# GEGLU feed-forward on one core: two small reads ahead of ScalarE's first block of x

## The chip, the cores and the metric

The kernel runs on one core of a Trainium2 chip. A core has five engines with instruction streams of their own: TensorE (PE, matmuls; its weight loads are shown apart as PEld), VectorE (DVE), ScalarE (ACT), GpSimd (POOL) and SyncE (SP), which here only starts transfers. Transfers started by SP and by ScalarE go through one DMA queue each (q1 and q10 in the profile); GpSimd's go through q0. All of them are carried out by the core's 16 DMA engines. Engines order themselves by semaphores. The metric is device time in microseconds, the median of several runs; less is better.

## What is computed

x has 1024 rows of 1024 (32 x 32 tokens), w_gate and w_up are 1024 x 3584, w_down is 3584 x 1024, all in bf16:

```python
def reference(x, w_gate, w_up, w_down):
    return (_gelu(x @ w_gate) * (x @ w_up)) @ w_down
```

`_gelu` is the tanh form of GELU.

## The kernel before

Every instruction stream is written out by hand: one function for each engine (`prog_sp`, `prog_act`, `prog_pool`, `prog_pe`, `prog_dve`) issues its instructions in order, and `wait` puts a semaphore wait ahead of the next one. There is no scheduler; the order on an engine is the order of the text. Each group of transfers has a semaphore of its own, wrapped in a `_Clock` that counts to 16 for one transfer.

*The work.* The hidden dimension, 3584, is cut into 28 chunks of 128 (`m`); the contraction over 1024 into 8 steps of 128 (`dk`). TensorE multiplies a 128 x 128 tile of weights with up to 512 columns of the transposed x (`xT`) and collects the 8 steps in a PSUM bank, once for the gate (G) and once for the up projection (U) (L388). ScalarE puts GELU on G (L446), VectorE multiplies it with U into `hT` (L486). After all chunks, TensorE runs the second product from `hT` and `wd` (L425), and ScalarE and VectorE take turns at copying the result out.

*The start.* x comes with its rows on the partitions and must be transposed. The first 256 rows come as two blocks of 128 rows and 256 KB, `xa[:, 0]` by SP and `xa[:, 1]` by ScalarE (L293, in `early_loads`, whose argument `side` is 0 for SP and 1 for ScalarE). For `dk` 0 to 4 TensorE transposes them by multiplying with an identity matrix (L355, `turn_xa`), in the order: block 0 for dk 0 to 2, block 1 for dk 0 to 2, block 0 for dk 3 and 4, block 1 for dk 3 and 4; ScalarE copies the three results from PSUM to `xT` (L439). For `dk` 5 to 7 VectorE transposes both blocks in 16 instructions (L462), after waiting for both. Ahead of this, TensorE runs seven matmuls of 512 columns on constants (`WARM`, L402), whose result is not used.

*The early weights.* After its block of x, SP starts the first 1024 columns (8 chunks) of both weight tensors, one `dk` at a time: wg and wu for k = 0, then for k = 1, and so on (L289, `load_w0`), 256 KB each, the last pair in halves. The weight tensors are laid out with 8 consecutive rows on each partition, so block k takes from every partition's group of 8 rows the row k. TensorE's first real matmuls are the 8 chunks for dk = 0 on the first 256 columns of x, in an order of parts and keys that follows the PSUM banks that the transposes leave free; then dk = 1 to 5 for all 8 chunks, and so on.

*The rest of x.* The remaining rows of x are started as six pieces by SP and six by ScalarE (L284, `load_x`), once the wu block for k = 5 has landed; on ScalarE they stand behind the three copies of L439. VectorE transposes them (L477). Later weights are started by SP (wg) and GpSimd (wu), L278 and L272.

At its end SP waits for the last output transfer.

Of the kernel before, what the change touches and what calls it, by code (L numbers as in the profile page):

```python
# [5 lines left out]
P = 128  # L6
BF16 = mybir.dt.bfloat16
# [77 lines left out]
def bass_standalone__geglu_ffn__sampling_kernel(  # L85
# [119 lines left out]
    def evac_eng_is_act(ji):  # L205
        return ji % 2 == 0
# [18 lines left out]
    Q_WD_SP = _Clock("wd_sp", 16)  # L225
    Q_WD_POOL = _Clock("wd_pool", 16)
    Q_OUT = _Clock("out", 16)
    all_clocks = [C_PE, C_ACT, C_DVE, C_POOL, *Q_XA, *Q_X.values(), *Q_W0.values(), *Q_W7.values(), *Q_WG, *Q_WU,
                  Q_WD_SP, Q_WD_POOL, Q_OUT]

    ctx = _Ctx()

    with ExitStack() as es:
        def sb(name, shape, dtype):
            return es.enter_context(nc.sbuf_tensor(name, shape, dtype))
# [11 lines left out]
        w_r = {"wg": wg_r, "wu": wu_r}  # L247
        NTB = 4
        t_bufs = [sb(f"tb{i}", [P, 512], FP32) for i in range(NTB)]
        warm = sb("warm", [P, 2], FP32)  # L250
        assert TC * D == DK * N
        osb = xT
        ps = es.enter_context(nc.psum_tensor("ps", [P, 8, 512], FP32))
# [13 lines left out]
        def issue_wd(ew, eng, mine, upto_chunk, clock, force=False):  # L267
            for k in list(mine):
                if force or wd_gate_chunk[k] <= upto_chunk:
                    ew.wait(C_PE, ctx.get(("U", last_part[wd_gate_chunk[k]])))  # L270
                    a, b = wd_groups[k]
                    ew.do(lambda: eng.dma_start(wd[:, a:b, :], wd_r[:, a:b, :]), clock=clock)  # L272
                    mine.remove(k)

        def load_w(ew, eng, w, j):
            c0, gsz, buf = groups[j]
            q = (Q_WG if w == "wg" else Q_WU)[j]
            ctx.set((w, j), ew.do(lambda: eng.dma_start(  # L278
                wbuf(w, buf)[:, :, 0:gsz * P], w_r[w][:, :, c0 * P:(c0 + gsz) * P]), clock=q))

        def load_x(ew, eng, q, side):
            c0, c1 = q[0] // 32, q[1] // 32
            for a in (2 * side, 2 * side + 1):
                v = ew.do(lambda: eng.dma_start(  # L284
                    xs[32 * a:32 * (a + 1), c0:c1, :], x_r[a, :, c0:c1, :]), clock=Q_X[(q, side)])
            ctx.set(("x", q, side), v)

        def load_w0(ew, eng, w, k, f0, f1, q):
            ctx.set((w + "0", k, f0), ew.do(lambda: eng.dma_start(  # L289
                big[w][:, k, f0:f1], w_r[w][:, k, f0:f1]), clock=q))  # L290

        def early_loads(ew, eng, side):
            ctx.set(("xa", side), ew.do(lambda: eng.dma_start(  # L293
                xa[:, side, :], xa_r[:, side, :]), clock=Q_XA[side]))
            yield
            if side == 0:
                for k in range(DK - 1):
                    for w in ("wg", "wu"):
                        load_w0(ew, eng, w, k, 0, NBIG * P, Q_W0[(w, k)])
                for h in range(2):  # L300
                    for w in ("wg", "wu"):
                        load_w0(ew, eng, w, DK - 1, h * GSZ * P, (h + 1) * GSZ * P,
                                Q_W7[w] if h else Q_W0[(w, DK - 1)])
            ew.wait(Q_W0[("wu", 5)], ctx.get(("wu0", 5, 0)))
            for q in XPIECES:
                load_x(ew, eng, q, side)

        def gate_w(ew, j):
            if war[j] is None:
                for s in range(2):  # L310
                    ew.wait(Q_X[(XC2, s)], ctx.get(("x", XC2, s)))
                return -1
            ew.wait(C_PE, ctx.get(("U", last_part[war[j]])))
            return war[j]
# [15 lines left out]
        def prog_sp(eng):  # L330
            sp = _Eng(ctx, eng, None)
            for _ in early_loads(sp, eng, 0):
                pass
            wd_mine = [k for k in range(len(wd_groups)) if k % 2 == 0]
            for j in range(NG):
                known_chunk = gate_w(sp, j)
                load_w(sp, eng, "wg", j)
                issue_wd(sp, eng, wd_mine, known_chunk, Q_WD_SP)
            issue_wd(sp, eng, wd_mine, FM, Q_WD_SP, force=True)
            ctx.set("wd_sp_total", Q_WD_SP.n)  # L340
            last = None
            for ji, (tc, col0, ncols, b) in enumerate(jobs):
                sp.wait(C_ACT if evac_eng_is_act(ji) else C_DVE, ctx.get(("E", ji)))
                last = sp.do(lambda: eng.dma_start(
                    out_r[:, tc, col0:col0 + ncols],
                    osb[:, tc, col0:col0 + ncols]), clock=Q_OUT)
            sp.wait(Q_OUT, last)

        def turn_xa(pe, eng, b, dk):
            pe.wait(Q_XA[b], ctx.get(("xa", b)))  # L350
            j = next(j for j, (_, k0, k1) in enumerate(XA_PS) if k0 <= dk < k1)
            bank, k0, k1 = XA_PS[j]
            o = 256 * (dk - k0) + P * b
            last = dk == k1 - 1 and b == 1
            v = pe.do(lambda: eng.matmul(  # L355
                ps[:, bank, o:o + P],
                xa[:, b, :].rearrange("p (j k) -> p j k", k=DK)[:, :, dk],
                ident[:, :], start=(dk == k0 and b == 0), stop=last), mark=last)
            if last:
                ctx.set(("XP", j), v)  # L360
# [72 lines left out]
        def prog_act(eng):  # L433
            act = _Eng(ctx, eng, C_ACT)
            act.do(lambda: eng.activation(warm[:, 0:1], const0, ACTF.Gelu_apprx_tanh))
            for _ in early_loads(act, eng, 1):
                for j, (bank, k0, k1) in enumerate(XA_PS):
                    act.wait(C_PE, ctx.get(("XP", j)))
                    ctx.set(("XA", j), act.do(lambda: eng.activation(  # L439
                        xT[:, k0:k1, XA[0]:XA[1]],  # L440
                        ps[:, bank, 0:256 * (k1 - k0)].rearrange("p (k t) -> p k t", t=256), ACTF.Copy)))
            for i, (m, t0, t1, (gb, g0, g1), us) in enumerate(parts):
                act.wait(C_PE, ctx.get(("U" if us[0] == gb else "G", i)))
                if i >= NTB:
                    act.wait(C_DVE, ctx.get(("D", i - NTB)))
                ctx.set(("A", i), act.do(lambda: eng.activation(  # L446
                    t_bufs[i % NTB][:, 0:t1 - t0], ps[:, gb, g0:g1], ACTF.Gelu_apprx_tanh)))
            for ji, (tc, col0, ncols, b) in enumerate(jobs):
                if not evac_eng_is_act(ji):
                    continue  # L450
                act.wait(C_PE, ctx.get(("O", ji)))
                ctx.set(("E", ji), act.do(lambda: eng.activation(  # L452
                    osb[:, tc, col0:col0 + ncols], ps[:, b, 0:ncols], ACTF.Copy)))

        def prog_dve(eng):
# [38 lines left out]

        progs = [
            (prog_sp, nc.sync, "sync"),
            (prog_act, nc.scalar, "scalar"),
            (prog_pool, nc.gpsimd, "gpsimd"),
# [45 lines left out]
```

## Time and profile before

| | |
|---|---|
| median of 3 runs | 299.84 us (299.69 to 299.94) |
| the profiled execution | 299.69 us |
| its span, first to last instruction | 298.4 us |
| TensorE busy | 294.2 us, 99% |
| VectorE, ScalarE, GpSimd busy | 64.3, 42.2, 7.9 us |
| moved from and to memory | 24.12 MB read, 2.10 MB written |
| ScalarE's queue, q10 | 1776 packets, 1.05 MB |

The span leaves out what lies ahead of the first and behind the last instruction, 1.3 us here. TensorE is busy for nearly all of the span; the row of busy tenths in 40 slices shows it at 9 (90% or more) in all but the first slice (8) and the last (7). A matmul is pipelined, so the length given for one is longer than the distance to the next one; distances between starts tell the rate. Rows of the timeline that end in `q` (SPq, ACTq) are the issues of transfers, and their length is the time that issuing takes, not that of the transfer.

### The profile page before, as it was taken

The page shows a single profiled execution, that of the slowest core. Times are in us where ns is not written, and L with a number is a line of the kernel's source. Part 1 is how long each engine was busy: PE and PEld are TensorE (multiplying, and loading weights), DVE is VectorE, ACT ScalarE, POOL GpSimd, SP SyncE. Part 2 cuts the span into 40 slices and gives each one's busy share as a digit, 9 for nine tenths or more (in the row PEclk, how much of TensorE's full clock was granted, in tenths as well). Part 3 has the DMA queues.
Part 4 walks back from the last instruction along what each step waited for, and adds up shares of the span by engine and source line. Part 5 has one row for each costly group of instructions (what it writes and reads, how often), then busy time and mean ns, then how long its engine had stood idle before and what let it go on. Part 6 is the DMA issues. An engine that isn't in the chain of part 4 may idle for free.

```text
span 298.4 us, 3487 instructions
## 1 busy us (share of the span) xinstructions
PE 294.2 (99%) x1525; PEld 149.3 (50%) x1549; DVE 64.3 (22%) x108; ACT 42.2 (14%) x78; POOL 7.9 (3%) x14
## 2 busy tenths in 40 slices
PE   8999999999999999999999999999999999999997
PEld 5899644444444444444444444444444444444446
DVE  4669722111122111122111112110000000000000
ACT  3032211121111121111112111110000000000000
POOL 1001001020001002001000000000000000000000
PEclk9999999999999999999999999999999999999999
DMA  7997104856008301942104000000000100010001
GB/s 255 386 205 234 51 2 125 296 181 244 0 0 295 129 0 27 371 167 93 49 0 141 0 2 0 0 0 20 18 18 18 37 18 18 20 35 18 18 20 35
DMA packets 18094, 26.43 MB, mean 89 GB/s; under 512 B 1056, under 2 KB 11936, under 8 KB 18080
## 3 DMA queue, kind: packets, MB, share of 16 engines
q1 hardware_dynamic: 14128, 16.78, 17.3%
q0 software_dynamic: 2176, 8.39, 7.9%
q10 hardware_dynamic: 1776, 1.05, 1.4%
q8 instruction: 12, 0.20, 0.3%
q14 instruction: 2, 0.02, 0.0%
HBM read 24.12 MB, written 2.10 MB: 88 GB/s over the span
## 4 chain that ended last, share of the span: by engine, by line
PE 99%; issue 0%; ACT 0%
PE ps L388 65%; PE ps L425 32%; PE ps L402 1%; PE ps L355 0%; ACT xT L452 0%
## 5 line engine op out<-in xcount | busy, mean ns | idle before, releaser
L425 PE MATMUL ps<-wd,hT 128*128 128x512 bf16 (+1 forms) x468 | 96.5, 366 | 0.4
L388 PE MATMUL ps<-xT,wgbig 128*128 128x512 bf16 (+2 forms) x394 | 79.6, 337 | 0.3
L388 PE MATMUL ps<-xT,wubig 128*128 128x512 bf16 (+2 forms) x395 | 79.5, 336 | 0.3
L425 PEld LDWEIGHTS ps<-wd,hT 128*128 128x128 bf16 x476 | 46.6, 98 | 50.4
L486 DVE TENSOR_TENSOR hT<-tb,ps 128x512 bf16<-128x512 f32 (+1 forms) x64 | 38.9, 615 | 136.6 <-PE ps L388 136.6
L446 ACT ACTIVATE tb<-ps 128x512 f32<-128x512 f32 (+1 forms) x64 | 34.2, 544 | 158.3 <-PE ps L388 155.4
L388 PEld LDWEIGHTS ps<-xT,wgbig 128*128 128x128 bf16 x400 | 38.3, 98 | 31.7 <-DMA wgbig<-in_w_gate_dram 0.2
L388 PEld LDWEIGHTS ps<-xT,wubig 128*128 128x128 bf16 x400 | 38.1, 98 | 31.4
L388 PE MATMUL ps<-xT,wgsmall 128*128 128x512 bf16 x126 | 30.1, 379 | 0.1
L388 PE MATMUL ps<-xT,wusmall 128*128 128x512 bf16 x125 | 29.8, 379 | 0.2
L492 DVE CAST xT<-ps 128x512 bf16<-128x512 f32 (+1 forms) x8 | 5.3, 658 | 88.1 <-PE ps L425 88.1
L388 PEld LDWEIGHTS ps<-xT,wgsmall 128*128 128x128 bf16 x128 | 12.5, 98 | 15.1
L388 PEld LDWEIGHTS ps<-xT,wusmall 128*128 128x128 bf16 x128 | 12.5, 98 | 15.1
L452 ACT ACTIVATE xT<-ps 128x512 bf16<-128x512 f32 (+1 forms) x9 | 5.2, 573 | 93.1 <-PE ps L425 93.1
L477 DVE STREAM_TRANSPOSE xT<-hT 128x128 bf16<-128x128 bf16 (+2 forms) x20 | 13.4, 705 | 0.0
L462 DVE STREAM_TRANSPOSE xT<-hT 32x192 bf16<-32x192 bf16 x16 | 8.2, 514 | 4.7 <-DMA hT<-in_x_dram 4.2
L278 POOL DMA_DIRECT2D wubig<-in_w_up_dram x3 | 2.7, 884 | 62.9 <-PE ps L388 62.9
L402 PE MATMUL ps<-const-bfloat16-1.0 128*128 128x512 bf16 x7 | 3.1, 627 | 0.8 <-PEq L529 0.8
L278 POOL DMA_DIRECT2D wusmall<-in_w_up_dram x2 | 2.0, 993 | 47.9 <-PE ps L388 26.0
L272 POOL DMA_DIRECT2D wd<-in_w_down_dram x3 | 2.3, 766 | 19.1 <-PE ps L388 19.1
L402 PEld LDWEIGHTS ps<-const-bfloat16-1.0 128*128 128x128 bf16 x7 | 0.9, 139 | 2.1 <-issue 2.1
L439 ACT ACTIVATE xT<-ps 128x512 bf16<-128x512 f32 (+1 forms) x3 | 1.4, 527 | 2.4 <-PE ps L355 2.4
(10 smaller groups left out, 4.9 us busy)
## 6 DMA issues: line engine op xcount, KB each, us to landing
wd<-in_w_down_dram SPq DMA_DIRECT2D x4, 1024.0 KB, 11.3
wgbig<-in_w_gate_dram SPq DMA_DIRECT2D x3, 1024.0 KB, 5.8
wubig<-in_w_up_dram POOLq DMA_DIRECT2D x3, 1024.0 KB, 9.6
wd<-in_w_down_dram POOLq DMA_DIRECT2D x3, 1024.0 KB, 11.3
wgsmall<-in_w_gate_dram SPq DMA_DIRECT2D x2, 1024.0 KB, 5.9
wusmall<-in_w_up_dram POOLq DMA_DIRECT2D x2, 1024.0 KB, 9.7
out_dram<-xT SPq DMA_DIRECT2D x15, 128.0 KB, 1.7
wgbig<-in_w_gate_dram SPq DMA_DIRECT2D x7, 256.0 KB, 5.3
```

Source lines behind the costliest of these rows:

```text
L272: ew.do(lambda: eng.dma_start(wd[:, a:b, :], wd_r[:, a:b, :]), clock=clock)
L278: ctx.set((w, j), ew.do(lambda: eng.dma_start(wbuf(w, buf)[:, :, 0:gsz * P], w_r[w][:, :, c0 * P:(c0 + gsz) * P]), clock=q))
L388: v = pe.do(lambda: eng.matmul(ps[:, bank, f0:f1], wbuf(w, buf)[:, dk, slot * P:(slot + 1) * P], xT[:, dk, t0:t1], start=first, stop=last ...
L402: pe.do(lambda: eng.matmul(ps[:, 0, 0:n], ones_w, ones_x[:, 0:n], start=True, stop=True), mark=False)
L425: v = pe.do(lambda: eng.matmul(ps[:, b, 0:ncols], hT[:, m, tc * P:(tc + 1) * P], wd[:, m, col0:col0 + ncols], start=(m == 0), stop=(m == F ...
L439: ctx.set(("XA", j), act.do(lambda: eng.activation(xT[:, k0:k1, XA[0]:XA[1]], ps[:, bank, 0:256 * (k1 - k0)].rearrange("p (k t) -> p k t", ...
L446: ctx.set(("A", i), act.do(lambda: eng.activation(t_bufs[i % NTB][:, 0:t1 - t0], ps[:, gb, g0:g1], ACTF.Gelu_apprx_tanh)))
L452: ctx.set(("E", ji), act.do(lambda: eng.activation(osb[:, tc, col0:col0 + ncols], ps[:, b, 0:ncols], ACTF.Copy)))
L462: v = dve.do(lambda: eng.transpose(xT[32 * a:32 * (a + 1), XA_DVE[0]:XA_DVE[1], XA[0]:XA[1]].rearrange("p k (b t) -> p k b t", t=P)[:, :, ...
L477: v = dve.do(lambda: eng.transpose(xT[:, dk, q[0]:q[1]].rearrange("p (c i) -> p c i", i=32), src))
L486: ctx.set(("D", i), dve.do(lambda: eng.tensor_tensor(hT[:, m, t0:t1], t_bufs[i % NTB][:, 0:t1 - t0], ps[:, ub, u0:u1], ALU.mult)))
L492: ctx.set(("E", ji), dve.do(lambda: eng.tensor_copy(osb[:, tc, col0:col0 + ncols], ps[:, b, 0:ncols])))
```

## The change

On ScalarE's side, `early_loads` first starts two small transfers: the first 16 columns (32 bytes) of each of the 128 rows of block k = 0 of `w_up`, then the same of `w_gate`, into a new small tile `probe`. Nothing reads this tile. Only then is ScalarE's block of x started. The order of the text on ScalarE is thus: the activation that loads the table, probe of `w_up`, probe of `w_gate`, block 1 of x, the three copies, the later pieces of x. The two transfers share a new semaphore, and SP waits for it at the very end, behind its wait for the last output. The rows read are those of the first wu and wg blocks that SP starts behind its own block of x. No other instruction is added, removed or moved.

```diff
+    Q_PROBE = _Clock("probe", 16)
     all_clocks = [C_PE, C_ACT, C_DVE, C_POOL, *Q_XA, *Q_X.values(), *Q_W0.values(), *Q_W7.values(), *Q_WG, *Q_WU,
-                  Q_WD_SP, Q_WD_POOL, Q_OUT]
+                  Q_WD_SP, Q_WD_POOL, Q_OUT, Q_PROBE]
...
+        probe = sb("probe", [P, 2, 16], BF16)
...
         def early_loads(ew, eng, side):
+            if side == 1:
+                for i, w in enumerate(("wu", "wg")):
+                    v = ew.do(lambda: eng.dma_start(probe[:, i, :], w_r[w][:, 0, 0:16]), clock=Q_PROBE)
+                ctx.set("probe", v)
             ctx.set(("xa", side), ew.do(lambda: eng.dma_start(
                 xa[:, side, :], xa_r[:, side, :]), clock=Q_XA[side]))
             yield
...
             sp.wait(Q_OUT, last)
+            sp.wait(Q_PROBE, ctx.get("probe"))
```

## The prediction, made before the changed kernel had run

> **What bounds the kernel now.** I read the chain of waits first. It is TensorE from end to end, so the time is the moment at which TensorE begins to run without a break, plus a fixed row of matmuls.
>
> ```profile
> PE 99%; issue 0%; ACT 0%
> PE ps L388 65%; PE ps L425 32%; PE ps L402 1%; PE ps L355 0%; ACT xT L452 0%
> ```
>
> Idle time in front of L388 and L425 is 0.1 to 0.4 us per group on the page. No later stall can be gained back, so only the first microseconds can move, and I read those next, in the timeline (start, length, engine, line, operation).
>
> ```profile
> 0.73 0.39 SPq L293 DMA_DIRECT2D hT<-in_x_dram  x1
> 0.77 3.15 PE L402 MATMUL ps<-const-bfloat16-1.0 128*128 128x512 bf16 x7 [0.77 <-PEq L529]
> 0.78 0.38 ACTq L293 DMA_DIRECT2D hT<-in_x_dram  x1
> ...
> 1.17 0.42 SPq L289 DMA_DIRECT2D wgbig<-in_w_gate_dram  x1
> ...
> 1.64 0.42 SPq L289 DMA_DIRECT2D wubig<-in_w_up_dram  x1
> ...
> 3.96 1.03 PEld L355 LDWEIGHTS ps<-ident,hT 128*128 128x128 bf16 x10 [0.96 <-issue]
> ...
> 4.24 8.13 DVE L462 STREAM_TRANSPOSE xT<-hT 32x192 bf16<-32x192 bf16 x15 [4.24 <-DMA hT<-in_x_dram]
> ...
> 4.65 1.36 ACT L439 ACTIVATE xT<-ps 128x256 bf16<-128x256 f32 x3 [2.43 <-PE ps L355]
> ...
> 5.18 1.08 PEld L388 LDWEIGHTS ps<-xT,wgbig 128*128 128x128 bf16 x7 [0.18 <-DMA wgbig<-in_w_gate_dram]
> ...
> 7.26 0.86 PEld L388 LDWEIGHTS ps<-xT,wgbig 128*128 128x128 bf16 x8
> ```
>
> Seven warm-up matmuls fill TensorE until 3.92. From 3.96 it transposes x (L355): rows of block 0 (SP's), then of block 1 (ScalarE's), dk 0 to 2 of each, then dk 3 and 4. ScalarE copies the first product out from 4.65 to 5.03, and the first real matmul starts at 5.18. When the blocks land is in the DMA view of 1.16 to 2.43 us (last column: us from issue to landing):
>
> ```profile
> q1 hardware_dynamic: 40, 0.08, 39.5%
> issues: line engine op xcount, KB each, median us to landing
> ...
> hT<-in_x_dram ACTq DMA_DIRECT2D x1, 256.0 KB, 3.4
> wubig<-in_w_up_dram SPq DMA_DIRECT2D x1, 256.0 KB, 4.2
> ```
>
> ScalarE's block of x lands at 0.78 + 3.4 = 4.18, and wu's k=0 block at 1.64 + 4.2 = 5.84. The first wg block has the shortest landing of that tile, 4.0 us, so 1.17 + 4.0 = 5.17, just before the start at 5.18. Narrow windows of the weight loads put the fourth transpose, the first that needs block 1, at 4.20. So block 1 has no slack to its own use, and the chain behind it has about 0.10 us: the copy ends at 5.03, TensorE could go on at 5.08, and it waits for wg until 5.18.
>
> One more thing is in these rows. The granted clock reads 1.00 in every stretch, but the starts do not: the warm-up loads follow each other by 0.42 us for 512 columns, while at 7.26 eight matmuls of 256 columns take 0.87 us, or 109 ns each. Narrow windows of the first L388 loads show 0.21 us for 256 columns up to 6.02 and half of that from there:
>
> ```profile
> 5.59 0.36 PEld L388 LDWEIGHTS ps<-xT,wgbig 128*128 128x128 bf16 x2
> ...
> 5.80 0.35 PEld L388 LDWEIGHTS ps<-xT,wgbig 128*128 128x128 bf16 x2
> ...
> 6.02 0.25 PEld L388 LDWEIGHTS ps<-xT,wgbig 128*128 128x128 bf16 x2
> ```
>
> TensorE thus runs at half rate until about 6.05, 5.28 us after its first matmul and after a spell with under 0.4 us of idle time in it.
>
> **The change, part by part.** *Two more DMA issues on ScalarE's queue.* SP's issues start 0.46 us apart (1.17, 1.64, 2.10), so block 1 is issued at 0.78 + 2 x 0.46 = 1.70 and not at 0.78. ScalarE itself has nothing to do until 4.65 but its table load, so the issues cost it nothing directly. Behind them on the queue come only block 1, the copies of L439, and the later pieces of x (held until 12.7 by a weight landing).
>
> *Whom block 1 now stands behind.* The issue order was SP x, ScalarE x, wg, wu. It becomes SP x, probe wu, wg (1.17), probe wg (1.24), wu (1.64), ScalarE x (1.70). Does ScalarE's queue wait for SP's older transfers? The row that shows it is at 12.71, where both queues issue pieces of x at the same moment, SP behind six blocks of weights still under way, ScalarE behind nothing:
>
> ```profile
> 12.71 3.90 SPq L284 DMA_DIRECT2D hT<-in_x_dram  x6
> 12.71 3.91 ACTq L284 DMA_DIRECT2D hT<-in_x_dram  x6
> ```
>
> The DMA view of 12.71 to 14.6 holds 643 packets of q1 (SP) and none of q10 (ScalarE); in 14.6 to 15.4 both move:
>
> ```profile
> q1 hardware_dynamic: 643, 0.68, 108.0%
> ...
> q1 hardware_dynamic: 269, 0.14, 76.2%
> q10 hardware_dynamic: 146, 0.07, 38.5%
> ```
>
> ScalarE's empty queue waited 1.9 us, as long as SP's own. The start agrees: SP's block of x moves its first packets 1.0 us after its issue, ScalarE's, issued 0.05 us later, has none before 2.43. I read this as service in the order of issue over both queues. Block 1 then moves from second to fourth place among blocks of 256 KB, the place that lands at 5.84. The probes add 256 packets, 16 for each DMA engine. Their price is not in the trace; between the 4-byte packets (9 ns) and the 512-byte ones (27 to 35 ns) it is 0.14 to 0.55 us, and I take 0.2, nearer to the small ones. Against this, two neighbours on different queues interleave (the two x blocks landed 0.3 us apart, where weight blocks are 0.67 apart), so I take off 0.3: 5.84 + 0.2 - 0.3 = 5.7. Ends: 4.7 (no service in issue order, below) and 6.4 (no interleaving, dear probes).
>
> [...]
>
> *TensorE's start.* Block 1 is 5.7 - 4.18 = 1.52 late; 0.10 of it is taken by the slack, so the first real matmul starts 1.42 later, at 6.60. wg has landed by then. The 0.87 us of work that TensorE did at half rate between 5.18 and 6.05 was worth 0.43 us at full rate; if the full rate still came at 6.05, the net loss would be 1.42 - 0.43 = 0.99 us.
>
> *The half rate.* TensorE now stands idle from 4.32 (three transposes of block 0) to 5.76, inside the spell that led to the full rate. No row shows what such a gap does. Below: idle time merely does not count, and the full rate comes 1.52 later, at 7.57; from 6.60 that is 0.97 us at half rate, a loss of 0.49. Above: the 5.28 us begin anew at 5.76 and end at 11.04; 4.44 us at half rate, a loss of 2.22. I take the middle, 9.3: 2.70 us, a loss of 1.35. The sum is 0.99 + 1.35 = 2.34 us.
>
> [...]
>
> *What stays hidden.* DVE's 16 transposes (L462) start with block 1 as well, 4.24 to about 5.8, and end at 14.5 instead of 12.95. TensorE needs them for dk=5 at 14.2 before, which moves to 16.5 in the forecast and to 15.2 at the least delay of 0.99; if that cover were gone, TensorE would wait for the difference. ScalarE's three copies then end at 7.53, and the matmuls that need the last one come 1.5 us behind the first at half rate, so about 8.1. Weight blocks and the other pieces of x move by the probes alone, 0.2 us, against over 1 us of new slack. SP's last wait finds its semaphore long reached: 0 to 0.05 us (one "issue" step of the chain), taken as 0.
>
> The profiled execution took 299.69 us with a span of 298.4; the forecast span is 300.7, that execution 302.0. The median is 0.15 above it, so 302.2 us.
>
> **The rivals.**
> 1. *Queues share, block 1 is hardly late* (not slower). Place: ScalarE's DMA queue. Its packets start 1.0 us after its issue as SP's first did, at 2.7 instead of 2.43, and it lands at 4.7 to 5.1 because q1 takes every second turn. The start slips 0.4 to 0.8 us, all within the half-rate spell, which halves it: 0.2 to 0.4, so 300.1. For it: 0.3 us between the two landings at the start. Against it: 12.71. It decides as long as block 1 lands before about 5.3; at that landing the loss reaches 0.6.
> 2. *Block 1 is late, but the full rate comes at 6.05 all the same*: + 0.99, 300.8. For it: nothing in the trace counts idle time. Against it: warm-up work alone, up to 3.92, did not bring the full rate, so a spell is being judged.
> 3. *The spell begins anew*: 0.99 + 2.22 = 3.21, 303.1.
> 4. *The early reads help the first weight blocks*. In 4.8 to 5.2 the DMA engines moved 246 GB/s and not the 385 of 2.43 to 3.1, so wg's landing could come sooner. TensorE waits for wg only 0.10 us, so this can't give more than 299.7, and only if block 1 were not late. This is also why a clear gain has almost no room.
>
> **How the numbers follow.** Forecast (302.2, with its own range 301.3 to 302.9) 0.45; rival 1 0.17; rival 2 0.24; rival 3 0.10; rival 4 or anything faster 0.04. 0.2% of 300 us is 0.6 us, about what a measurement of this kernel can tell from no change. Slower by more: forecast, rivals 2 and 3, 0.79. Within: rival 1, 0.17. Faster: 0.04. The range reaches from rival 1's lower part, 299.9, to rival 3, 303.1.
>
> **What would show it.** In the changed trace: ScalarE's block of x issued at about 1.7 and landed at 5.4 to 6.0, behind or beside wu's first block; the DVE transposes starting with it; a gap in TensorE between the third and the fourth L355; the first L388 near 6.6; the pitch of 0.21 us lasting to about 9.3; from there on every start later by about 2.3, and no new idle time. I am wrong if block 1 lands before 5.1, if the pitch of 0.109 us is there from the first L388 on, or if the end does not move with the start.

## The result and the profile after

The changed kernel takes 304.16 us (303.96 to 304.59, 4 runs); the kernel before, run beside it, 299.76 us. The ratio is 1.0153 (95% interval 1.0133 to 1.0172): slower by 4.4 us. The forecast was 302.2, with a range up to 303.1. The profiled execution took 304.31 us with a span of 303.0, 4.6 us above the span before.

The chain of waits of the changed kernel, by engine and by line:

```profile
PE 97%; DMA 2%; issue 0%; ACT 0%; ACTq 0%
PE ps L395 64%; PE ps L432 32%; DMA hT<-in_x_dram 2%; PE ps L362 0%; ACTq L297 0%; ACT L442 0%; ACT xT L459 0%
```

New in it is the transfer of x, 2% of the span, and the issue of the early reads (ACTq L297) ahead of it. The warm-up matmuls, 1% before, are gone from the chain: TensorE now waits behind them. The timeline of the start (start, length, engine, line, operation), where the lines of TensorE, of VectorE and of ScalarE's copies stand 7 numbers higher than before (L388 is now L395), those of the loads 2 or 6 (L289 is L291, L293 is L299):

```profile
0.78 0.39 ACTq L297 DMA_DIRECT2D probe<-in_w_up_dram  x1
...
1.17 0.42 SPq L291 DMA_DIRECT2D wgbig<-in_w_gate_dram  x1
1.21 0.46 ACTq L297 DMA_DIRECT2D probe<-in_w_gate_dram  x1
...
1.64 0.42 SPq L291 DMA_DIRECT2D wubig<-in_w_up_dram  x1
1.69 0.45 ACTq L299 DMA_DIRECT2D hT<-in_x_dram  x1
...
3.55 0.43 PEld L362 LDWEIGHTS ps<-ident,hT 128*128 128x128 bf16 x3 [0.55 <-issue]
...
7.09 0.72 PEld L362 LDWEIGHTS ps<-ident,hT 128*128 128x128 bf16 x7 [3.11 <-DMA hT<-in_x_dram]
...
7.15 7.03 DVE L469 STREAM_TRANSPOSE xT<-hT 32x192 bf16<-32x192 bf16 x13 [7.15 <-DMA hT<-in_x_dram]
...
7.95 1.20 PEld L395 LDWEIGHTS ps<-xT,wgbig 128*128 128x128 bf16 x7
...
11.13 1.60 PEld L395 LDWEIGHTS ps<-xT,wgbig 128*128 128x128 bf16 x8
...
12.74 0.86 PEld L395 LDWEIGHTS ps<-xT,wubig 128*128 128x128 bf16 x8
```

Block 1 is issued at 1.69, as forecast, and TensorE stands still for 3 us between the third and the fourth transpose. The first real matmul starts at 7.98, 2.79 later than before. Eight weight loads take 1.60 us at 11.13 and 0.86 us at 12.74: the half rate lasts until about 12.64, where before it ended at 6.08. From this the 4.6 us can be added up: 2.79 later, plus (12.64 - 7.98)/2 = 2.33 lost at half rate, less the (6.08 - 5.19)/2 = 0.45 that was lost so before: 4.67.

How the 16 shares of block 1 came in is in the DMA views of 4.1 to 5.6 and of 5.6 to 7.1 us (packets, MB, share of the 16 engines):

```profile
q1 hardware_dynamic: 152, 0.28, 53.4%
q10 hardware_dynamic: 137, 0.25, 49.8%
...
q1 hardware_dynamic: 285, 0.52, 99.8%
q10 hardware_dynamic: 10, 0.02, 2.9%
```

ScalarE's queue (q10) has its first packet of x at 4.19, 2.5 us after its issue. From there its packets move beside SP's in nearly equal numbers, 137 against 152 in this view, and nearly all of the block (0.25 MB) has moved by 5.6; 14 of the 16 shares have landed at 5.88. The last ten packets come one by one between 285 of SP's weight packets, and the two last shares land at 6.57 and 7.04.

### The profile page after: what moved, and what is told of

It is laid out like the page before. It is cut to its first block, busy times and chain, and to the rows that moved or that the text cites. A ratio compares the mean times of both kernels' runs of the same rounds, so it can differ in the third digit from the quotient of the medians.

```text
span 303.0 us, 3489 instructions
## 1 busy us (share of the span) xinstructions
PE 296.1 (98%) x1525; PEld 150.2 (50%) x1549; DVE 64.2 (21%) x108; ACT 42.2 (14%) x78; POOL 7.9 (3%) x14
## 4 chain that ended last, share of the span: by engine, by line
PE 97%; DMA 2%; issue 0%; ACT 0%; ACTq 0%
PE ps L395 64%; PE ps L432 32%; DMA hT<-in_x_dram 2%; PE ps L362 0%; ACTq L297 0%; ACT L442 0%; ACT xT L459 0%
## 5 line engine op out<-in xcount | busy, mean ns | idle before, releaser
L432 PE MATMUL ps<-wd,hT 128*128 128x512 bf16 (+1 forms) x468 | 96.5, 367 | 0.4
L395 PE MATMUL ps<-xT,wgbig 128*128 128x512 bf16 (+2 forms) x394 | 80.7, 341 | 0.3
L395 PE MATMUL ps<-xT,wubig 128*128 128x512 bf16 (+2 forms) x395 | 80.5, 339 | 0.3
L432 PEld LDWEIGHTS ps<-wd,hT 128*128 128x128 bf16 x476 | 46.6, 98 | 50.4
L395 PEld LDWEIGHTS ps<-xT,wgbig 128*128 128x128 bf16 x400 | 38.7, 99 | 32.2 <-DVE xT L484 0.2
L395 PEld LDWEIGHTS ps<-xT,wubig 128*128 128x128 bf16 x400 | 38.5, 99 | 31.9
L395 PE MATMUL ps<-xT,wgsmall 128*128 128x512 bf16 x126 | 30.1, 379 | 0.1
L395 PE MATMUL ps<-xT,wusmall 128*128 128x512 bf16 x125 | 29.8, 379 | 0.2
L395 PEld LDWEIGHTS ps<-xT,wgsmall 128*128 128x128 bf16 x128 | 12.5, 98 | 15.1
L395 PEld LDWEIGHTS ps<-xT,wusmall 128*128 128x128 bf16 x128 | 12.5, 98 | 15.1
L459 ACT ACTIVATE xT<-ps 128x512 bf16<-128x512 f32 (+1 forms) x9 | 5.2, 573 | 93.1 <-PE ps L432 93.1
L484 DVE STREAM_TRANSPOSE xT<-hT 128x128 bf16<-128x128 bf16 (+2 forms) x20 | 13.3, 697 | 0.0
L362 PE MATMUL ps<-ident,hT 128*128 128x128 bf16 x10 | 1.5, 313 | 2.9 <-DMA hT<-in_x_dram 2.9
L362 PEld LDWEIGHTS ps<-ident,hT 128*128 128x128 bf16 x10 | 1.1, 161 | 3.7 <-DMA hT<-in_x_dram 3.1
```

Of the source, the lines that this page charges most:

```text
L362: v = pe.do(lambda: eng.matmul(ps[:, bank, o:o + P], xa[:, b, :].rearrange("p (j k) -> p j k", k=DK)[:, :, dk], ident[:, :], start=(dk == ...
L395: v = pe.do(lambda: eng.matmul(ps[:, bank, f0:f1], wbuf(w, buf)[:, dk, slot * P:(slot + 1) * P], xT[:, dk, t0:t1], start=first, stop=last ...
L432: v = pe.do(lambda: eng.matmul(ps[:, b, 0:ncols], hT[:, m, tc * P:(tc + 1) * P], wd[:, m, col0:col0 + ncols], start=(m == 0), stop=(m == F ...
L459: ctx.set(("E", ji), act.do(lambda: eng.activation(osb[:, tc, col0:col0 + ncols], ps[:, b, 0:ncols], ACTF.Copy)))
L484: v = dve.do(lambda: eng.transpose(xT[:, dk, q[0]:q[1]].rearrange("p (c i) -> p c i", i=32), src))
```

## The experiments

In all of them "first and last share" are the landing times of the first and last of block 1's 16 shares, "start" is the first real matmul and "full rate" the time from which 256 columns take 0.11 us, each in the one profiled execution, which is not always a typical one: it took 300.23 us in e5, 302.06 in e7, 302.26 in e6 and 301.56 in e11, against the medians in the last column. Run times are medians, with the kernel before beside them on the same chip (299.28, 299.44, 299.81 and 299.48 in the four sets, in the order told).

| kernel | issue of block 1 | first and last share | start | full rate | run, us |
|---|---|---|---|---|---|
| before | 0.78, second | 3.81, 4.14 | 5.19 | 6.08 | 299.76 |
| changed | 1.69, behind wg, wu | 5.37, 7.04 | 7.98 | 12.64 | 304.16 |
| e1, reads of 16 rows | 1.67, behind wg, wu | 5.73, 7.73 | 8.62 | 11.64 | 304.02 |
| e2, no reads, late issue | 1.72, behind wg, wu | 5.41, 7.92 | 8.85 | 10.86 | 304.32 |
| e3, reads behind block 1 | 0.78, second | 3.87, 4.21 | 5.10 | before it | 299.57 |
| e4, longer warm-up | 1.69, behind wg, wu | 5.38, 7.05 | 7.94 | before it | 301.97 |
| e5, one read | 1.21, behind wg | 4.54, 5.30 | 6.19 | before it | 301.42 |
| e6, weights held to 1.7 | 1.68, with wg | 4.97, 6.10 | 7.04 | 9.51 | 303.03 |
| e7, SP issues both | second, by SP | 3.81, 4.24 | 6.30 | 9.86 | 299.92 |
| e8, short warm-up | 0.78, second | 3.88, 4.18 | 5.12 | 7.60 | 300.53 |
| e9, one queue, fourth | 2.10, behind wg, wu | 5.17, 6.83 | 7.72 | 11.15 | 303.76 |
| e10, later weights held | 1.69, behind wg, wu | 5.32, 5.85 | 6.79 | 9.06 | 302.10 (one run) |
| e11, late, weights behind | 1.71, second | 4.28, 5.07 | 6.01 | 9.12 | 302.36 |
| e12, e9 with the reads | 2.10, behind wg, wu | 5.30, 6.66 | 7.55 | 10.42 | 302.66 |
| e13, e2, later weights held | 1.72, behind wg, wu | 5.22, 6.14 | 7.03 | before it | 303.05 (one run) |

**e1: fewer packets in the reads.**

```diff
-                    v = ew.do(lambda: eng.dma_start(probe[:, i, :], w_r[w][:, 0, 0:16]), clock=Q_PROBE)
+                    v = ew.do(lambda: eng.dma_start(probe[0:16, i, :], w_r[w][0:16, 0, 0:16]), clock=Q_PROBE)
```

> The two early reads take 16 rows each and not 128 (one packet for each DMA engine); their place and their two issues stay. Theory 'order of issue': block 1 is still issued at 1.7 behind wu, most of it lands at 5.4 to 5.9, and the span stays 2.3 to 4.7 us above the 298.4 of before. Theory 'small packets': the 256 packets of 32 bytes cost the time, so block 1 lands before 5.0 and the span is at most 1 us above before.

304.02 us, ratio 1.0163 (1.0134 to 1.0192). Block 1 comes even later than I expected: eleven of its 16 shares land after 6.0. With an eighth of the packets nothing is gained (304.16 us with all of them); the packets of the reads are not what costs.

**e2: no reads, the same late issue.**

```diff
         def early_loads(ew, eng, side):
+            if side == 1:
+                ew.wait(C_POOL, ctx.get("ident"))
```

> The kernel before, without any early read; ScalarE waits for GpSimd's identity matrix (done at 1.69) and issues block 1 then, at about 1.75. Theory 'order of issue': the same as in the changed kernel, block 1 lands at 5.4 to 7.0, run 302.2 to 304.3. Theory 'the reads themselves are what costs': block 1 lands before 5.0, run at most 300.8.

304.32 us, ratio 1.0166 (1.0146 to 1.0186). The whole loss is there without a single early read; the last share, 7.92, is well beyond my range for the theory of the order, and the time just beyond it. The timeline of this kernel shows one issue on ScalarE's queue and the same standstill (L357 is its L355):

```profile
1.72 0.40 ACTq L295 DMA_DIRECT2D hT<-in_x_dram  x1
3.44 0.54 PEld L357 LDWEIGHTS ps<-ident,hT 128*128 128x128 bf16 x3 [0.43 <-issue]
7.96 0.72 PEld L357 LDWEIGHTS ps<-ident,hT 128*128 128x128 bf16 x7 [3.98 <-DMA hT<-in_x_dram]
```

**e3: the same reads behind block 1.**

```diff
+            ctx.set(("xa", side), ew.do(lambda: eng.dma_start(
+                xa[:, side, :], xa_r[:, side, :]), clock=Q_XA[side]))
             if side == 1:
                 for i, w in enumerate(("wu", "wg")):
...
-            ctx.set(("xa", side), ew.do(lambda: eng.dma_start(
-                xa[:, side, :], xa_r[:, side, :]), clock=Q_XA[side]))
```

> The same two early reads of 128 rows, on ScalarE's queue behind block 1 and not ahead of it. Theory 'order of issue': block 1 lands at 4.1 to 4.3 as before, run 299.5 to 300.1. Theory 'small packets': the 256 packets hold up wg and wu on the same engines, wg lands after 5.5, run above 300.5. If early reads of a weight tensor help its first block, wg lands before 5.0, but the run gains at most 0.1.

299.57 us, ratio 1.0008 (0.9999 to 1.0018), no difference. Its timeline has the ten transposes without a gap again:

```profile
0.78 0.38 ACTq L295 DMA_DIRECT2D hT<-in_x_dram  x1
1.20 0.46 ACTq L299 DMA_DIRECT2D probe<-in_w_up_dram  x1
1.68 0.45 ACTq L299 DMA_DIRECT2D probe<-in_w_gate_dram  x1
4.00 0.76 PEld L362 LDWEIGHTS ps<-ident,hT 128*128 128x128 bf16 x10 [1.00 <-issue]
```

With block 1 ahead of them (last share at 4.21), the two reads in the queue cost nothing in these runs: 299.57 us against 299.28. wg landed at 4.93 and not 5.14 in this trace, which may be a help of the reads to the first weights; the run does not show it.

**e4: the gap filled.**

```diff
-        WARM = [512] * 7
+        WARM = [512] * 17
```

> The changed kernel with 17 and not 7 warm-up matmuls, so that TensorE has no gap ahead of block 1. Theory 'the spell begins anew': without the gap the full rate comes at 6.0 to 6.4, first L388 near 8.0 at full rate, span 300.6 to 301.2, run 301.9 to 302.5. Rival 'the full rate depends on when real work starts, or on a fixed time of this kernel': the rate changes at 12 to 13 us all the same and the span stays at 303.

301.97 us, ratio 1.0089 (1.0074 to 1.0104). Block 1 lands exactly as in the changed kernel (last share at 7.05 and 7.04), and the start is the same; only the clock differs. So the half rate is worth 303.0 - 300.7 = 2.3 us of span, and the lateness itself the other 2.3 (300.7 - 298.4; of the 2.75 us by which the start is later, 0.45 are the half rate of the kernel before). The full rate came at 4.67 in this trace and not at 6.0 to 6.4, so the theory named in the expectation, that a spell of one length begins anew, is not confirmed by its number. The first loads of L395 in this kernel's timeline, 7 in 0.67 us where the changed kernel needs 1.20:

```profile
7.09 0.52 PEld L362 LDWEIGHTS ps<-ident,hT 128*128 128x128 bf16 x7 [0.52 <-DMA hT<-in_x_dram]
7.91 0.67 PEld L395 LDWEIGHTS ps<-xT,wgbig 128*128 128x128 bf16 x7 [0.30 <-issue]
```

**e5: one read only.**

```diff
-                for i, w in enumerate(("wu", "wg")):
+                for i, w in enumerate(("wg",)):
```

> The changed kernel with the read of w_gate alone, so that block 1 is issued once later and not twice, at about 1.21: behind wg (1.17), ahead of wu (1.64). Theory 'order of issue': third place, most of block 1 lands at 4.8 to 5.4, a few engines later; run 300.5 to 303.5, between before and the change. Theory 'any read ahead of block 1 costs the whole': run at 304 again.

301.42 us (300.1 to 302.24), ratio 1.0059 (1.0038 to 1.0080). One place less far back, and issued 0.48 earlier, block 1 is complete 1.74 earlier. The cost is smaller, 301.42 us against the 304.16 of the change; the place and the issue time, which this kernel moves together, cannot be told apart in it. The runs fall into two groups, four at 300.1 to 300.4, the profiled one among them, and six at 301.3 to 302.2.

**e6: SP's weights held until block 1 is issued.**

```diff
             if side == 0:
+                ew.wait(C_POOL, ctx.get("ident"))
                 for k in range(DK - 1):
```

> The changed kernel with both reads, where SP waits for GpSimd's identity matrix (1.69) ahead of its first weights: block 1 is still issued at about 1.7, but wg at about 1.74 and wu at 2.2, both behind it. Theory 'order of issue': block 1 is second of the large blocks again and lands at 4.1 to 4.8; wg lands at 5.1 to 5.7; run 299.3 to 300.8. Theory 'the time of the issue alone': block 1 lands after 5.3 again; run above 302.

303.03 us, ratio 1.0113 (1.0083 to 1.0143). The theory of the order missed both its numbers: block 1 came 0.9 earlier than in the change but not at 4.1 to 4.8. By its last share, 6.10, and its time, the run is what I had written for the other theory, the time of the issue alone. But the two issues, 1.68 and 1.70, were a tie, so the kernel did not put block 1 clearly ahead and does not decide between them. e11 does put it ahead.

**e7: SP issues both blocks, ScalarE only the reads.**

```diff
-            ctx.set(("xa", side), ew.do(lambda: eng.dma_start(
-                xa[:, side, :], xa_r[:, side, :]), clock=Q_XA[side]))
+            for b in range(2):
+                if side == 0:
+                    ctx.set(("xa", b), ew.do(lambda: eng.dma_start(
+                        xa[:, b, :], xa_r[:, b, :]), clock=Q_XA[b]))
```

> SP issues both blocks of x, then the weights; ScalarE issues the two reads of 128 rows and no block. Theory 'order of issue': block 1, issued at 1.17 right behind block 0, lands at 4.0 to 4.5, weights one issue later (wg at 5.1 to 5.5); run 299.1 to 300.0, the reads cost nothing that can be measured. Theory 'the reads slow whatever moves beside them': block 1 lands after 5, run above 301.

299.92 us, ratio 1.0027 (1.0001 to 1.0053). Block 1 is on time (4.24), with both reads in flight. Seven of the ten runs lie at 299.4 to 300.6 and three at 301.5 to 302.6; the profiled one is of these: there the last share of wg lands at 6.26 and not 5.14, and TensorE waits for it. So "the reads cost nothing" holds for block 1 and not always for wg, which here is issued 0.47 later too.

**e8: a gap on TensorE alone.**

```diff
-        WARM = [512] * 7
+        WARM = [512] * 3
```

(in the kernel before)

> The kernel before with 3 and not 7 warm-up matmuls, so TensorE is idle from about 2.1 to 3.96 while all transfers stay. It tests the clock alone. Theory 'a spell of 3.4 us, laid out independently of the kernel, must be mostly busy': the full rate comes at 6.4 to 9.9, differently in each run, first L388 still at 5.2; span up by 0.2 to 1.9 us, run 299.6 to 301.4, and more spread than before. Rival 'idle time before the first real matmul is harmless': rate changes at 6.1 or earlier, run 299.1 to 299.9.

300.53 us (300.01 to 301.34), ratio 1.0030 (1.0017 to 1.0044). The landing of block 1 and the start are nearly those of the kernel before; the full rate comes at 7.60 and not at 6.08, and the time goes up by 1.1 us. So idle time on TensorE that delayed nothing (the start is 5.12, against 5.19) cost 1.1 us here, by the clock.

**e9: the same place on one queue.**

```diff
+            def load_xa(s):
+                ctx.set(("xa", s), ew.do(lambda: eng.dma_start(
+                    xa[:, s, :], xa_r[:, s, :]), clock=Q_XA[s]))
+            if side == 0:
+                load_xa(0)
...
                     for w in ("wg", "wu"):
                         load_w0(ew, eng, w, k, 0, NBIG * P, Q_W0[(w, k)])
+                    if k == 0:
+                        load_xa(1)
```

(in the kernel before; its own issue of `xa` is taken out)

> The kernel before without reads, where SP issues everything early on its one queue in the order block 0, wg, wu, block 1, then the other weights; ScalarE issues no block. It gives block 1 the place that the change gave it, without a second queue. Theory 'order of issue, and on top of it the sharing of DMA engines between two queues': all of block 1 lands at 5.3 to 5.9, its last share within 0.6 of the first; run 301.2 to 302.8. Theory 'fourth place alone costs the whole': last share after 6.5, run 303.5 or more.

303.76 us, ratio 1.0139 (1.0112 to 1.0166). My theory of two queues fell: without a second queue the last share still lands at 6.83. Its issue, at 2.10, is 0.41 later here than in the changed kernel, so place and time are not quite the same.

**e10: the changed kernel with the weights from k=1 on held until block 1 has landed.**

```diff
                 for k in range(DK - 1):
+                    if k == 1:
+                        ew.wait(Q_XA[1], ctx.get(("xa", 1)))
```

> The changed kernel, where SP holds the weights from k=1 on until block 1 has landed. Only the landing of block 1 is of interest, since TensorE then waits for the held weights; the time will be longer. Theory 'SP's later blocks take turns with block 1 on the DMA engines': its last share lands at 5.0 to 5.8, within 0.6 of the first. Rival 'the reads or the late issue delay some engines by themselves': the last share still lands after 6.5.

All shares between 5.32 and 5.85, 0.05 past my range: the late ones are gone.

**e11: late issue, weights clearly behind.** As e2, and SP waits for ScalarE's first activation:

```diff
             if side == 0:
+                ew.wait(C_ACT, ctx.get("warm"))
                 for k in range(DK - 1):
```

> No reads; ScalarE issues block 1 at about 1.72 as in the second experiment, and SP waits for ScalarE's first activation (2.2) ahead of its first weights, so block 1 is clearly second in order. Theory 'order of issue': block 1 lands at 3.8 to 4.7 although it is issued as late as in the changed kernel; wg lands at 4.9 to 5.7; run 299.2 to 301. Theory 'the time of its issue': lands after 5.3, run above 302.

Block 1 lands at 4.28 to 5.07, against 5.41 to 7.92 in e2 with the same issue time. The last share is 0.93 later than before, just what the issue is (1.71 against 0.78). The run, 302.36 (ratio 1.0088, 1.0069 to 1.0107), is longer than I expected: the start slips to 6.01, and the full rate comes at 9.12. The last share, 5.07, is past the 4.7 of the one theory and short of the 5.3 of the other, and the time, above 302, is the one I had written for the other. So both count: the order, since e2 with the same issue lands 2.85 later, and the time of the issue, which costs 0.93 in this trace. The DMA views of 2.8 to 3.2 and of 3.2 to 3.5 us show that ScalarE's queue moves nothing until 3.2, although next to nothing else moves from 2.8 on:

```profile
q1 hardware_dynamic: 12, 0.00, 4.0%
...
q10 hardware_dynamic: 19, 0.04, 35.6%
```

**e12 and e13: what makes the last shares late.** e12 is e9 with the two reads of 128 rows on ScalarE; e13 is e2 with the hold of e10.

> As the one-queue kernel (SP: block 0, wg, wu, block 1), but ScalarE also issues the two reads of 128 rows at its start. Theory 'the first packets of the weights are served slowly, and reads of all 128 rows ahead of them take that up': block 1 lands at 5.0 to 6.1, its last share within 0.7 of the first, earlier than without the reads (6.83), run 301.3 to 303.0. Theory 'fourth place alone': last share after 6.5, run 303.4 to 304.4.

> No reads, block 1 issued by ScalarE at about 1.72 behind wg and wu, SP's weights from k=1 on held until block 1 has landed. Only the landing is of interest. Theory 'the first packets of the weights are served slowly': fewer than 60 blocks of 2 KB per half microsecond between 3.5 and 4.5, last share of block 1 after 6.2. Theory 'only taking turns with later weights': last share before 6.0 as with the reads (5.85).

e12: last share at 6.66, against 6.83 without the reads; 302.66 us, ratio 1.0098 (1.0077 to 1.0120). e13: last share at 6.14, between the two expectations, with 352 GB/s between 3.5 and 4.5, where e2 had 213. Slow first packets that reads take up do not explain the late shares by themselves: the reads changed the last share by 0.17 in e12, and the low rate was absent in e13 without any reads. A smaller help of the reads is not excluded: e12's time lies in the range of that theory and 1.1 us below e9's, though the intervals of the two ratios overlap, and of the kernels in which ScalarE issues block 1, those with reads of 128 rows (7.04 and 7.05) have it complete ahead of e1 and e2 (7.73, 7.92). What goes with late shares is that SP's next weights follow at once: in the six kernels where block 1 is behind wg and wu and they follow, the last share lands at 6.66 to 7.92; in the two where they are held, at 5.85 and 6.14. Each of these is one trace. Late shares are not a matter of block 1 alone: wu, which is ahead of it, has its last share at 7.73 in e2, 7.53 in e1, 6.82 in e4 and 6.17 in e9, against 5.81 before, and in e7 three shares of wg are late while block 1 is on time. Why shares come late when later transfers follow, on one queue too, stays open; DMA engine numbers are not in these traces.

**The clock, from all of these.** In some executions the record holds the granted clock of the start. Stretches of 3.41 us of e1 (length, busy time of PE, PEld, DVE, ACT, POOL, granted clock, DMA share, GB/s), then of the changed kernel, where the clock column is not filled for this part and the distances between starts tell the rate:

```profile
1.40:4.81 3.41, 2.92 (x9) 0.88 (x7) 0.00 (x0) 0.80 (x2) 0.28 (x1) 1.00 0.86 221
4.81:8.22 3.41, 0.44 (x7) 0.45 (x7) 0.39 (x1) 0.12 (x1) 0.00 (x0) 1.00 0.98 330
8.22:11.63 3.41, 3.27 (x19) 2.18 (x18) 3.20 (x7) 1.24 (x3) 0.00 (x0) 0.50 1.05 404
11.64:15.05 3.41, 3.41 (x33) 3.06 (x32) 3.22 (x7) 0.00 (x0) 0.00 (x0) 1.00 1.06 375
```

```profile
2.40:5.81 3.41, 1.83 (x7) 0.71 (x5) 0.00 (x0) 0.00 (x0) 0.00 (x0) 1.00 1.05 324
5.81:9.22 3.41, 2.13 (x14) 1.60 (x15) 1.98 (x4) 1.36 (x3) 0.00 (x0) 1.00 1.02 386
9.22:12.63 3.41, 3.41 (x18) 2.35 (x17) 3.19 (x8) 0.00 (x0) 0.00 (x0) 1.00 1.05 395
```

In e1 the full rate is granted at 4.81 after a stretch in which TensorE was busy for 2.92 us of 3.41, is taken back at 8.22 after one with 0.44, and comes back at 11.64. In e2 (4.04 to 7.45), e9 (4.33 to 7.74) and e12 (3.6 to 7.0) it is also granted for about 3.41 us and taken back; the granted clock of the stretch behind, 7.45 to 10.86 in e2 and 7.74 to 11.15 in e9, is 0.50. In the changed kernel, with stretches of this length laid out backwards from 12.64, two in a row, 1.83 and 2.13 us busy, did not bring it; the third, 3.41 us busy, did. Laid out backwards from the change of rate in the other traces, a stretch with 2.52 us of 3.41 (e11) did not bring it, and one with 2.89 (e2) did; it was lost after 0.81 (e12) and kept after 1.75 (e13). The ends of matmuls are modelled in a profile, so these busy times are approximate. The changes of rate, and so the stretches, lie at another moment in each of these traced executions: 8.22 and 11.64 in e1, 7.45 and 10.86 in e2, 7.74 and 11.15 in e9, 12.64 in the changed kernel. That the same kernel therefore pays differently from run to run is an inference: the two groups of e5 fit it, but each kernel was traced only once.

## Why the prediction was off

*What bounds the kernel, and the direction:* right. The time moved with the start of the real matmuls and with the rate, and nothing was gained or lost later; idle in front of L395 and L432 stays at 0.1 to 0.4 us per group.

*The issue at 1.70:* right (1.69). *Place in the order:* right as a cause, but not the only one. e3 and e7 keep block 1 second with the reads in flight and have it at 4.2; e2 loses it without reads; e5 lies between; e11 gets it back only to 5.07 with the late issue. By these traces the 2.90 us by which the last share is late divide into 0.93 for the later issue in itself (e11), 0.78 for standing behind wg and wu (e10 against e11, which has no reads) and 1.19 for the weights that follow (the change against e10). The two rows from which I read service in the order of issue also say less than I took from them: in e11 ScalarE's first packet came 1.5 us after its issue with the DMA engines nearly idle at the end (4.0% in 2.8 to 3.2), so most of the 1.65 us at the start and of the 1.9 us at 12.71 may need no older transfer to explain it. *The probes' own 0.2 us:* not seen as a cost. e1 with an eighth of the packets and e2 with none are no faster; the 32-byte packets took 9 ns each, the low end of what I allowed.

*"5.84 + 0.2 - 0.3 = 5.7" for the landing of block 1:* the first term that was mis-sized. It landed at 7.04, beyond the upper end of 6.4. With the next weights held it lands at 5.85 (e10) and, without reads, at 6.14 (e13), not far from my sum; what I left out is the further 1.2 us (against e10) to 1.8 us (e2 against e13) by which the last shares come later when the next weights follow at once. The start came at 7.98 and not 6.60: 1.38 us too little. I had read the time of wu's landing as the price of fourth place, but wu's last share at 5.81, with the next weights behind it too, was no measure of block 1's slowest share at that place; why not stays open.

*"I take the middle, 9.3" for the end of the half rate:* the second term. It came at 12.64, beyond the upper end of 11.04, so 2.33 us were lost where I had put 1.35, 0.98 too little. 1.38 + 0.98 and the forecast 2.34 make 4.70, against 4.6 in the spans. The bound itself was built wrongly: "the 5.28 us begin anew at 5.76" took the time from the first matmul for a length that the chip counts, while the rate in e1 changed in steps of 3.41 us (4.81, 8.22, 11.64). With such steps laid out backwards from 12.64, the gap of the changed kernel ended at 7.09, inside the one from 5.81 to 9.22, and the half rate went on behind it, though TensorE was busy for 2.13 us of it. e4 shows the term by itself, 2.3 us.

Of the stretches of 3.41 us, one that was busy for 74% (2.52, e11) did not bring the full rate, and one that was busy for 85% (2.89, e2) did; no run shows more of how busy a stretch must be.

*The rivals.* Queues that share (rival 1) did not save block 1, though they do share once ScalarE's has packets of x: between 4.1 and 5.6 the queues of SP and ScalarE move 0.28 and 0.25 MB. But ScalarE's packets of x begin only at 4.19, where e11, with the same issue and the weights behind, has its first at 3.2. Rival 2 is excluded by the changed trace itself (12.64, not 6.05) and by e8. Rival 3, the dearest, came nearest to the time, by luck: 5.28 us from the end of the gap, 7.09, would be 12.37, close to the measured 12.64, but in e2 the same rule gives 7.96 + 5.28 = 13.24 where the full rate came at 10.86. Rival 4: no run with early reads was faster than the kernel before; a smaller help of the reads, in e12, is not excluded.

*What was hidden* stayed hidden: VectorE's transposes began with block 1 (7.15), and TensorE shows no wait for them; its one wait for VectorE, 0.2 us as before, is for the transposes of the later rows (L484).

No version beat the kernel before: e3, the best, cannot be told from it.

## What to carry to other kernels

That ScalarE's queue was empty did not make a transfer on it free here: two issues put ahead of a critical load made its issue 0.9 us later (1.69 against 0.78), behind two blocks of 256 KB that SP issued in that time, and with the blocks that follow them its last share landed at 7.04 and not at 4.14. Price such a move by the whole order of issues over all queues, and by the slowest share of the transfer (7.04), not by the typical one (14 of 16 by 5.88). And price a gap on TensorE during its start twice, once for the wait and once for the clock: here each was about 2.3 us, and a longer warm-up (e4) bought the second half back, 300.7 us of span against 303.0.

## What the runs showed of the hardware that was not expected

TensorE's full rate was granted and taken back 3.41 us apart (4.81, 8.22 and 11.64 in e1), at other moments in other traced executions (7.45 and 10.86 in e2, 7.74 and 11.15 in e9); four kernels lost a rate that they already had (e1, e2, e9, e12). ScalarE's transfer had its first packet 1.5 us after its issue even though the DMA engines stood nearly idle from 2.8 on (e11: issued at 1.71, none before 3.2; the other queue took 4.0% of the engines in 2.8 to 3.2), where SP's first needed 1.0 in the kernel before (0.73 to 1.74). And the 16 shares of block 1, which land within 0.33 us of each other in the kernel before (3.81 to 4.14), came up to 2.5 us apart (e2, 5.41 to 7.92).
